# Piecewise loads, query-first landmarks and earlier denominators in a fused Nyström attention and FFN kernel

## The chip, the core and the metric

The kernel runs on one core of a Trainium2 chip. Its time is the device time in microseconds, taken over several runs; one further execution is profiled. The engines are named as the profile names them: PE is TensorE (matrix multiplications; PEld is its loading of weights), DVE is VectorE, ACT is ScalarE, POOL is GpSimd, SP is SyncE. SP, ACT and POOL also issue DMA transfers. [...]

## What is computed

```python
# per batch (8) and head (8): q, k, v are 576 x 64; m = 32 landmarks, each the mean of 18 rows
q_lm, k_lm = means of q and of k over groups of 18 rows
A  = softmax(q @ k_lm.T / 8)          # 576 x 32
Bm = softmax(q_lm @ k_lm.T / 8)       # 32 x 32
C  = softmax(q_lm @ k.T / 8)          # 32 x 576
Z  = Bm.T / (norm1(Bm) * norminf(Bm) + 1e-6)
for _ in range(6):
    Z = 2 * Z - Z @ Bm @ Z
attn = A @ Z @ C @ v
# then, over all 4608 tokens of width 512 (the heads side by side):
x = attn
h = ((x @ w1) * (x @ w2)) @ w3        # w1, w2: 512 x 1024; w3: 1024 x 1024
out = h @ w_out                       # w_out: 1024 x 512
```

All inputs and the output are float32.

## The kernel before

**Folding.** No step between `w3` and `w_out` is nonlinear, so the kernel first multiplies the two (`fold`, in float32) into `w34`. This is a generator of 64 steps, one matrix multiplication each; the program takes steps of it between the parts of the first batch's work. In the same manner `x @ w1` is never formed from the attention's output: the 32-column product `Z C v` of every head is multiplied by that head's rows of `w1` and `w2` (`project`, which gives G, tile `gt`), and the normalised `A` (tile `ahat`) is multiplied by G (`up`).

**Loading and turning.** `load_qk` brings q and k of a batch in as float16 through POOL's queue (96 partitions, 8 heads of 384 elements each); `load_v` brings v in as float32 through SP's queue. `turn_all` issues four DMA transposes on SP's queue, which give `qkT`: the 64 head dimensions of the two row halves on 128 partitions. `w1` and `w2` come in on partitions 0 to 63 of `wdup`; `double_weight` repeats them on partitions 64 to 127.

**Landmarks.** `landmarks` adds groups of rows of `qkT`, for k and for q, by four additions each. The results `parts` hold sums of one half of the rows on partitions 0 to 63 and of the other half on 64 to 127. `exchange` swaps the halves by two DMA transfers on SP into `other`, and `combine` adds the two into `lm`, a float16 tile that holds the full sums in both halves.

**Attention.** `attention` is a generator with 13 yields: `qbd` and the scores of Bm (`psB`); the scores of C in two parts (`scores_c`), whose exponentials `ect` POOL adds up (`presum`); the scores of A (`scores_a`) and the products with v (`cv`); then six iterations of the inverse on `chain`. In iterations 3, 4 and 5 a third of the reciprocals of A's denominators is taken (`inverted`); `mixed` makes `rmix` of them, and `normalise` multiplies them into A.

**The order of the work** is written out by hand: the functions issue instructions where the program calls them, and a tile pool's buffers add waits. The main loop runs over the eight batches. In batch b's iteration there come first the transposes and v's load of batch b+2; then the up-phase, eight pairs of `up` for batch b with one step of the attention of batch b+1 in each pair; then q's and k's load of batch b+3 and the landmarks of batch b+2; then the d-phase, which takes `down` (the product with `w34`, and the output stores on SP) 8 or 10 times. The d-phase steps on through the attention of batch b+1 and, in its last two places, through `project`:

```python
            steps(at if n < nd - 2 else proj)
            if n == 3 and b + 2 < B:
                exchange(sts[b + 2])
                combine(sts[b + 2])
```

PSUM is held as three buffers `big` of two banks, one `small` and one `acc`.

Of the kernel before, what the change touches and what calls it, by code (L numbers as in the profile page):

```python
# [8 lines left out]
FP32 = mybir.dt.float32  # L9
FP16 = mybir.dt.float16  # L10
AXF = mybir.ActivationFunctionType
ALU = mybir.AluOpType
AX = mybir.AxisListType

B = 8
H = 8
# [10 lines left out]
NP = 96  # L27
# [4 lines left out]
def kernel(  # L32
# [11 lines left out]
    nc = tc.nc  # L44
    consts = ctx.enter_context(tc.tile_pool(name="consts", bufs=1))
    wpool = ctx.enter_context(tc.tile_pool(name="wpool", bufs=1))
    pin = ctx.enter_context(tc.tile_pool(name="pin", bufs=2))
    pat = ctx.enter_context(tc.tile_pool(name="pat", bufs=2))
# [7 lines left out]
    def small():  # L56
        return psp.tile([128, 512], FP32, name="small", bufs=1)
# [7 lines left out]
    w34 = wpool.tile([128, 8, DM], FP16, name="w34")  # L65


    def load_qk(st, b):
        qkn = pin.tile([128, 2, H, 384], FP16, name="qkn")
        for t, src in ((1, k), (0, q)):  # L70
            nc.gpsimd.dma_start(out=qkn[0:NP, t, :, :],
                                in_=src[b].rearrange("h (p r) d -> p h (r d)", p=NP))
        st["qkn"] = qkn

    def load_v(st, b):
        vt = pin.tile([128, H, 384], FP32, name="vt")
        nc.sync.dma_start(out=vt[0:NP], in_=v[b].rearrange("h (p r) d -> p h (r d)", p=NP))
        st["vt"] = vt

    def load_weight(t, w):  # L80
        nc.gpsimd.dma_start(out=wdup[0:64, :, t, :], in_=w.rearrange("(h d) j -> d h j", d=D))

    def double_weight(t):
        nc.sync.dma_start(out=wdup[64:128, :, t, :], in_=wdup[0:64, :, t, :])

    def transposes(st, t, hs):
        if "qkT" not in st:
# [47 lines left out]
        return mask4, par, ones, eye, onesq, selc, lomask  # L135


    def landmarks(st, turned=None):

        st["parts"] = parts = pz.tile([128, 2, H, 32], FP32, name="parts")  # L140

        def sums(t, h0, n, eng, pool):
            x = st["qkT"][:, 1 - t, h0:h0 + n, :, :]
            tr = pool.tile([128, n, NP], FP32, name="tr", bufs=1)
            eng.tensor_tensor(out=tr, in0=x[:, :, 0, :], in1=x[:, :, 1, :], op=ALU.add)  # L145
            eng.tensor_tensor(out=tr, in0=tr, in1=x[:, :, 2, :], op=ALU.add)  # L146
            t3 = tr.rearrange("p h (l g) -> p h l g", g=3)
            o = parts[:, t, h0:h0 + n, :]
            eng.tensor_tensor(out=o, in0=t3[:, :, :, 0], in1=t3[:, :, :, 1], op=ALU.add)
            eng.tensor_tensor(out=o, in0=o, in1=t3[:, :, :, 2], op=ALU.add)  # L150

        sums(1, 0, H, nc.gpsimd, pat)
        if turned is None:
            sums(0, 0, H, nc.gpsimd, pat)
        else:
            sums(0, 0, 4, *turned)
            sums(0, 4, 4, *turned)


    def exchange(st):  # L160
        st["other"] = pat.tile([128, 2, H, 32], FP32, name="other", bufs=1)
        nc.sync.dma_start(out=st["other"][0:64], in_=st["parts"][64:128])
        nc.sync.dma_start(out=st["other"][64:128], in_=st["parts"][0:64])

    def combine(st):
        st["lm"] = lm = pat.tile([128, 2, H, 32], FP16, name="lm")
        nc.gpsimd.tensor_tensor(out=lm, in0=st["parts"], in1=st["other"], op=ALU.add)  # L167


    chain = [consts.tile([128, 2, 3, 32], FP32, name=f"chain{i}") for i in range(2)]  # L170
# [3 lines left out]

    def attention(st, bank=None, vbank=None):
        bank, vbank = bank or small, vbank or small
        qkT, vt, lm = st["qkT"], st["vt"], st["lm"]
        qbd = pat.tile([128, H, 2, 32], FP16, name="qbd")
        nc.vector.tensor_tensor(
# [1 line left out]
            in0=lm[:, 0, :, :].unsqueeze(2).to_broadcast([128, H, 2, 32]),  # L181
            in1=par.unsqueeze(1).unsqueeze(3).to_broadcast([128, H, 2, 32]),
            op=ALU.mult)
        psB = small()
        for qd in range(2):
            for h in range(4):
                nc.tensor.matmul(psB[32 * h:32 * h + 32, 32 * qd:32 * qd + 32],
                                 lm[0:64, 0, 4 * qd + h, :], lm[0:64, 1, 4 * qd + h, :],
                                 start=True, stop=True, tile_position=(0, 32 * h))
        ebm = pz.tile([128, 2, 32], FP32, name="ebm")  # L190
        nc.scalar.activation(out=ebm, in_=psB[:, 0:64].rearrange("p (a m) -> p a m", m=32),
# [33 lines left out]

        scores_c(0)
        es0 = presum(0)
        yield
        scores_c(1)
        es1 = presum(1)  # L230
# [92 lines left out]
        def inverted(i):  # L323
            sl = slice(QS // 3 * i, QS // 3 * (i + 1))
            nc.vector.reciprocal(out=psS[:, 1, sl], in_=psS[:, 0, sl])  # L325
# [21 lines left out]
        for it in range(6):  # L347
            last = it == 5
            old, new = chain[it % 2], chain[1 - it % 2]
            psI = bank() if it < 3 else small()  # L350
            for qd in range(2):
                for h in range(4):
                    sl = slice(32 * h, 32 * h + 32)
                    nc.tensor.matmul(  # L354
                        psI[sl, 64 * qd + 32 * last:64 * qd + 64], old[sl, qd, 0, :],
                        old[sl, qd, 2, :] if last else old[sl, qd, 0:3:2, :],
                        start=True, stop=True, tile_position=(32 * h, 32 * h))
            pv_ = psI[:, 0:128].rearrange("p (a c m) -> p a c m", a=2, m=32)
            if not last:
                nc.vector.tensor_tensor(out=new[:, :, 0:3:2, :], in0=old[:, :, 1:3, :], in1=pv_,  # L360
                                        op=ALU.add)
            else:
                y = pz.tile([128, 2, 32], FP32, name="y")
                nc.vector.tensor_tensor(out=y, in0=old[:, :, 2, :], in1=pv_[:, :, 1, :], op=ALU.add)
                ybd = pz.tile([128, 2, 4, 32], FP32, name="ybd")
                nc.vector.tensor_tensor(
                    out=ybd, in0=y.unsqueeze(2).to_broadcast([128, 2, 4, 32]),
                    in1=mask4.unsqueeze(1).to_broadcast([128, 2, 4, 32]), op=ALU.mult)
            if it == 0:
                cv(0, 1, psV0, es0)  # L370
                scaled(0, psV0)
            elif it == 1:
                psV1 = vbank()
                cv(1, 0, psV1)
            elif it == 2:
                cv(1, 1, psV1, es1)
                scaled(1, psV1)
                psS = denominators()
            else:
                inverted(it - 3)  # L380
            yield
        rmix = mixed()
        psZ = small()
        for qd in range(2):
            nc.tensor.matmul(psZ[:, 128 * qd:128 * qd + 128],
# [117 lines left out]
    sts = [dict() for _ in range(B)]  # L503

    def turn_all(b):
        for t in (1, 0):
            for h0 in (0, 4):
                transposes(sts[b], t, range(h0, h0 + 4))

    def steps(g, n=1):  # L510
        for _ in range(n):
            next(g, None)


    gate = consts.tile([128, 1], FP32, name="gate")
    with tc.tile_pool(name="pf", bufs=2) as pf:
# [19 lines left out]
            nc.tensor.matmul(psw[:, 0, 0:256], warm[:, 0:128], warm, start=True, stop=True)  # L536

        nc.gpsimd.tensor_copy(out=gate, in_=wof[:, 2, 0:1])
        load_qk(sts[0], 0)
        load_w3(2)  # L540
        mask4, par, ones, eye, onesq, selc, lomask = constants()
        fd = fold(pf, wof, w3f)
        steps(fd, 5)
        load_w3(3)
        turn_all(0)
        load_v(sts[0], 0)
        steps(fd, 8)
        load_w3(4)
        landmarks(sts[0])
        load_weight(0, moe_w1)  # L550
        load_weight(1, moe_w2)
        load_qk(sts[1], 1)
        steps(fd, 8)
        load_w3(5)
        exchange(sts[0])
        combine(sts[0])
        steps(fd, 8)
        load_w3(6)
        steps(fd, 6)
        double_weight(0)  # L560
        at = itertools.chain(attention(sts[0], vbank=lambda: big()[:, 0, :]), project(sts[0]))
        for n in range(28):
            steps(at)
            if n == 4:
                load_w3(7)
                double_weight(1)
                turn_all(1)
                load_v(sts[1], 1)
            if n == 17:
                landmarks(sts[1], (nc.vector, pf))  # L570
                load_qk(sts[2], 2)
                exchange(sts[1])
                combine(sts[1])
            steps(fd)
        steps(at, 30)
        steps(fd, 64)
# [4 lines left out]
    for b in range(B):  # L581
        st = sts[b]
        ab = st["ab"] = pab.tile([128, 8, S], FP16, name="ab")
        if b + 2 < B:
            turn_all(b + 2)
            load_v(sts[b + 2], b + 2)
        if b % 2 == 0:
            chunks = [[(b, ab, 128 * t, 128)] for t in range(4)]
        else:
            chunks = [[(b - 1, sts[b - 1]["ab"], 512, 64), (b, ab, 0, 64)]]  # L590
            chunks += [[(b, ab, 64 + 128 * t, 128)] for t in range(4)]
        for j in range(8):
            up(st, j, 0)
            steps(at)
            up(st, j, 1)
        if b + 3 < B:
            load_qk(sts[b + 3], b + 3)
        if b + 2 < B:
            landmarks(sts[b + 2])
        proj = project(sts[b + 1]) if b + 1 < B else iter(())  # L600
        hold = {}
        nd = 2 * len(chunks)
        for n in range(nd):
            bank = (lambda: big()[:, 0, :]) if n // 2 % 2 else acc
            down(chunks[n // 2], n % 2, hold, bank)
            steps(at if n < nd - 2 else proj)
            if n == 3 and b + 2 < B:
                exchange(sts[b + 2])
                combine(sts[b + 2])
        at = attention(sts[b + 2], acc) if b + 2 < B else iter(())  # L610


# [28 lines left out]
```

## Time and profile before

| what | value |
|---|---|
| time, median of 13 runs | 313.31 us (307.72 to 318.05) |
| the profiled execution's own time | 311.22 us |
| its span, first to last instruction | 309.4 us |
| TensorE busy | 285.4 us |
| VectorE, ScalarE, GpSimd busy | 167.9, 113.0, 126.9 us |
| mean granted TensorE clock | 0.983 |
| DMA, mean rate over the span | 164 GB/s |

The rows of the profile's groups read: line, engine, operation, output and inputs by the program's names, shapes, count, then total busy microseconds and mean nanoseconds of one, then idle time before it and what ended it. In the table of windows each line has the stretch, its length, the busy time and the number of instructions of PE, PEld, DVE, ACT and POOL, and at its end the granted clock, the share of the 16 DMA engines and GB/s. In the list of waits the three figures are microseconds in total, number of times and longest. "issue" stands where an engine waited for nothing that the profile shows. The DMA queues are q0 (issued by POOL), q1 (issued by SP), q10 (issued by ACT), q8 and q14 (instructions).

### The profile page before, as it was taken

The page shows a single profiled execution, that of the slowest core. Times are in us where ns is not written, and L with a number is a line of the kernel's source. Part 1 is how long each engine was busy: PE and PEld are TensorE (multiplying, and loading weights), DVE is VectorE, ACT ScalarE, POOL GpSimd, SP SyncE. Part 2 cuts the span into 40 slices and gives each one's busy share as a digit, 9 for nine tenths or more (in the row PEclk, how much of TensorE's full clock was granted, in tenths as well). Part 3 has the DMA queues.
Part 4 walks back from the last instruction along what each step waited for, and adds up shares of the span by engine and source line. Part 5 has one row for each costly group of instructions (what it writes and reads, how often), then busy time and mean ns, then how long its engine had stood idle before and what let it go on. Part 6 is the DMA issues. An engine that isn't in the chain of part 4 may idle for free.

```text
span 309.4 us, 8609 instructions
## 1 busy us (share of the span) xinstructions
PE 285.4 (92%) x3632; PEld 157.6 (51%) x3632; DVE 167.9 (54%) x408; ACT 113.0 (37%) x193; POOL 126.9 (41%) x141
## 2 busy tenths in 40 slices
PE   7999979999999899699999998997899999999994
PEld 5454435444366456344664663465446644654651
DVE  6111124369077658364865775485368764865720
ACT  1010003042162276125723742473047326723632
POOL 0209514008159429901793396149414931400000
PEclk9999979999999999899999999999799999999999
DMA  7999999999999578954999799599848934003114
GB/s 232 322 250 207 225 246 240 247 142 206 200 194 217 127 119 157 231 119 129 139 243 212 147 182 205 138 156 220 134 127 160 183 94 114 2 4 102 36 42 130
DMA packets 68424, 50.89 MB, mean 164 GB/s; under 512 B 39969, under 2 KB 58401, under 8 KB 68385
## 3 DMA queue, kind: packets, MB, share of 16 engines
q1 hardware_dynamic: 53696, 36.71, 54.7%
q0 software_dynamic: 13600, 11.54, 24.3%
q10 hardware_dynamic: 1088, 2.10, 1.9%
q8 instruction: 28, 0.46, 0.7%
q14 instruction: 12, 0.09, 0.1%
HBM read 38.80 MB, written 9.44 MB: 156 GB/s over the span
## 4 chain that ended last, share of the span: by engine, by line
PE 62%; DMA 11%; DVE 10%; ACT 6%; issue 5%; POOL 4%; SPq 1%; ACTq 0%; POOLq 0%; DVEq 0%
PE big L423 20%; PE acc L443 12%; PE big L443 7%; PE acc L497 5%; DMA other<-parts 5%; PE small L262 4%; PE small L354 3%; PE big L409 3%; PE acc L354 3%; DMA wof<-in_moe_w_out_dram 2%; DMA qkn<-in_k_dram 2%; DVE gt L415 2%; DVE ab L429 2%; PE big L339 2%; ACT ect L211 2%
## 5 line engine op out<-in xcount | busy, mean ns | idle before, releaser
L423 PE MATMUL big<-ahat,gt 128*128 128x288 f16 x512 | 75.4, 289 | 2.7 <-ACT a_sb L427 1.0
L423 PEld LDWEIGHTS <-gt 128*128 128x128 f16 x512 | 46.6, 98 | 21.8 <-issue 7.8
L429 DVE TENSOR_TENSOR ab<-a_sb,big 128x576 f16<-128x576 f16 x64 | 48.1, 752 | 16.8 <-PE big L423 8.6
L427 ACT CAST a_sb<-big 128x576 f16<-128x576 f32 x64 | 40.8, 638 | 39.2 <-PE big L423 39.2
L497 PE MATMUL acc<-wof,w3t 128*128 128x512 f32 x96 | 48.0, 621 | 1.0 <-DMA wof<-in_moe_w_out_dram 0.4
L443 PE MATMUL acc<-w,ab 128*128 128x512 f16 (+1 forms) x192 | 42.0, 393 | 0.0
L443 PEld LDWEIGHTS <-ab 128*128 128x128 f16 (+1 forms) x320 | 25.8, 102 | 28.7 <-issue 5.6
L145 POOL TENSOR_TENSOR tr<-qkT 128x768 f32<-128x768 f16 x15 | 24.6, 1641 | 31.2 <-DMA qkT<-qkn 30.6
L415 DVE TENSOR_SCALAR gt<-big 128x512 f16<-128x512 f32 x32 | 20.6, 686 | 27.7 <-ACT gt L413 27.7
L167 POOL TENSOR_TENSOR lm<-parts,other 128x512 f16<-128x512 f32 x8 | 10.1, 1268 | 55.7 <-DMA other<-parts 55.7
L218 POOL TENSOR_TENSOR t<-ect 96x384 f32<-96x384 f32 x16 | 16.0, 999 | 40.0 <-ACT ect L211 39.3
L443 PE MATMUL big<-w,ab 128*128 128x512 f16 x128 | 32.2, 381 | 0.0
L449 ACT ACTIVATE o_sb<-acc 128x512 f32<-128x512 f32 x20 | 11.9, 597 | 54.4 <-PE acc L443 53.3
L146 POOL TENSOR_TENSOR tr<-tr,qkT 128x768 f32<-128x768 f32 x15 | 24.8, 1652 | 1.2
L473 DVE COPY w3t<-big 128x512 f32<-128x512 f32 (+1 forms) x15 | 8.5, 583 | 29.9 <-PE big L465 29.8
L497 PEld LDWEIGHTS acc<-wof,w3t 128*128 128x128 f32 x96 | 16.8, 195 | 14.9 <-issue 11.9
L413 ACT ACTIVATE gt<-big 128x512 f16<-128x512 f32 x32 | 17.8, 595 | 6.5 <-PE big L409 6.5
L262 PE MATMUL small<-vt,ect 96*32 96x64 f32 x672 | 15.7, 225 | 3.1 <-issue 3.1
L409 PE MATMUL big<-wdup,zt 128*32 128x512 f16 x256 | 17.4, 382 | 0.1
L449 ACT ACTIVATE o_sb<-big 128x512 f32<-128x512 f32 x16 | 9.6, 597 | 21.7 <-PE big L443 18.3
L354 PEld LDWEIGHTS small<-chain 32*32 32x32 f32 x432 | 6.9, 105 | 15.5 <-DVE big L325 8.1
L497 PE MATMUL small<-wof,w3t 128*128 128x512 f32 x32 | 14.7, 593 | 0.0
(98 smaller groups left out, 326.0 us busy)
## 6 DMA issues: line engine op xcount, KB each, us to landing
vt<-in_v_dram SPq DMA_DIRECT2D x8, 1152.0 KB, 9.2
qkn<-in_k_dram POOLq DMA_DIRECT2D x8, 576.0 KB, 9.5
qkn<-in_q_dram POOLq DMA_DIRECT2D x8, 576.0 KB, 13.3
out_dram<-o_sb SPq DMA_DIRECT2D x24, 192.0 KB, 2.3
w3f<-in_moe_w_dram SPq DMA_DIRECT2D x6, 512.0 KB, 9.7
out_dram<-o_sb SPq DMA_DIRECT2D x24, 128.0 KB, 2.4
wof<-in_moe_w_out_dram ACTq DMA_DIRECT2D x4, 512.0 KB, 7.8
wdup<-in_moe_w_dram POOLq DMA_DIRECT2D x2, 1024.0 KB, 13.5
```

What stands on the lines that cost most here:

```text
L145: eng.tensor_tensor(out=tr, in0=x[:, :, 0, :], in1=x[:, :, 1, :], op=ALU.add)
L146: eng.tensor_tensor(out=tr, in0=tr, in1=x[:, :, 2, :], op=ALU.add)
L262: nc.tensor.matmul(psV[32 * h:32 * h + 32, 0:64], ects[qd][0:NP, h, r, :], vt[0:NP, 4 * qd + h, 64 * r:64 * r + 64], start=(r == 0), stop= ...
L354: nc.tensor.matmul(psI[sl, 64 * qd + 32 * last:64 * qd + 64], old[sl, qd, 0, :], old[sl, qd, 2, :] if last else old[sl, qd, 0:3:2, :], sta ...
L409: nc.tensor.matmul(psG[32 * h:32 * h + 32, n, :], zt[:, 4 * qd + h, :], wdup[:, 4 * qd + h, w, 512 * n:512 * n + 512], start=True, stop=Tr ...
L415: nc.vector.tensor_scalar(out=dst[:, 1, :], in0=psG[:, 1, :], scalar1=1.0 / ZS, scalar2=None, op0=ALU.mult)
L423: nc.tensor.matmul(p[:, c, 0:HS], st["g"][qd][:, w, 128 * j:128 * j + 128], st["ahat"][qd][:, c, :], start=(qd == 0), stop=(qd == 1))
L427: nc.scalar.copy(out=st["a_sb"], in_=p[:, :, 0:HS])
L429: nc.vector.tensor_tensor(out=st["ab"][:, j, :].rearrange("p (c s) -> p c s", c=2), in0=st["a_sb"], in1=p[:, :, 0:HS], op=ALU.mult)
L443: nc.tensor.matmul(pso[o:o + sz, :], ab[:, j, s0:s0 + sz], w34[:, j, :], start=(j == 0), stop=(j == 7), tile_position=(0, o))
L449: nc.scalar.activation(out=o_sb, in_=pso[:, :], func=AXF.Copy, scale=1.0 / (X64 * X64))
L497: nc.tensor.matmul(psW[j][:, :], turned[j, cc][:, c4, :], wof[:, c, :], start=(c == 0), stop=(c == 7))
```

## The change

- q is loaded, turned and summed ahead of k. In the main loop, `load_qk` and `load_v` become generators that issue four pieces: q in two and k in two, one piece ahead of each of the two long additions of a landmark sum, on POOL's queue; v in four, among the stores of the d-phase, on SP's queue.
- `exchange` and `combine` work on q and on k separately; `combine` moves from POOL to DVE, into `attention`. Bm is multiplied from q's full sums and k's partial sums `kp` (a float16 copy of `parts`) over all 128 partitions, and no exchange of k stands ahead of it.
- Two thirds of the reciprocals are taken in iteration 3, the last third and `mixed` in iteration 4.
- `project` takes the last but two and the last but one place of the d-phase.
- `double_weight` is 16 ScalarE copies, where it was two DMA transfers on SP.
- For the second batch, all sums are made on POOL, at the fifth step of the first batch's attention (n = 4), where they were made partly on DVE at n = 17.

```diff
+    def load_qk(st, b, n=8):
+        st["qkn"] = qkn = pin.tile([128, 2, H, 384], FP16, name="qkn")
+        for t, src in ((0, q), (1, k)):
+            for h in range(0, H, n):
+                yield
+                nc.gpsimd.dma_start(out=qkn[0:NP, t, h:h + n, :],
+                                    in_=src[b, h:h + n].rearrange("h (p r) d -> p h (r d)", p=NP))
+    def load_v(st, b, n=8):
+        st["vt"] = vt = pin.tile([128, H, 384], FP32, name="vt")
+        for h in range(0, H, n):
+            yield
+            nc.sync.dma_start(out=vt[0:NP, h:h + n],
+                              in_=v[b, h:h + n].rearrange("h (p r) d -> p h (r d)", p=NP))
-    def double_weight(t):
-        nc.sync.dma_start(out=wdup[64:128, :, t, :], in_=wdup[0:64, :, t, :])
+    def double_weight(t, h):
+        nc.scalar.copy(out=wdup[64:128, h, t, :], in_=wdup[0:64, h, t, :])
...
+    def landmarks(st, loads=iter(())):
         st["parts"] = parts = pz.tile([128, 2, H, 32], FP32, name="parts")
+        steps(loads)
+        for t in range(2):
+            x = st["qkT"][:, 1 - t]
+            tr = pat.tile([128, H, NP], FP32, name="tr", bufs=1)
+            steps(loads)
+            nc.gpsimd.tensor_tensor(out=tr, in0=x[:, :, 0, :], in1=x[:, :, 1, :], op=ALU.add)
+            steps(loads)
+            nc.gpsimd.tensor_tensor(out=tr, in0=tr, in1=x[:, :, 2, :], op=ALU.add)
...
+        st["kp"] = kp = pat.tile([128, H, 32], FP16, name="kp")
+        nc.gpsimd.tensor_copy(out=kp, in_=parts[:, 1])
...
+    def combine(st, t):
+        if t == 0:
+            st["lm"] = pat.tile([128, 2, H, 32], FP16, name="lm")
+        nc.vector.tensor_tensor(out=st["lm"][:, t], in0=st["parts"][:, t], in1=st["other"][:, t],
+                                op=ALU.add)
...
     def attention(st, bank=None, vbank=None):
+        combine(st, 0)
...
-                                 lm[0:64, 0, 4 * qd + h, :], lm[0:64, 1, 4 * qd + h, :],
+                                 lm[:, 0, 4 * qd + h, :], st["kp"][:, 4 * qd + h, :],
...
         es0 = presum(0)
+        combine(st, 1)
         yield
...
-            else:
-                inverted(it - 3)
+            elif it == 3:
+                inverted(0)
+                inverted(1)
+            elif it == 4:
+                inverted(2)
+                rmix = mixed()
             yield
-        rmix = mixed()
...
         for n in range(28):
             steps(at)
             if n == 4:
                 load_w3(7)
-                double_weight(1)
                 turn_all(1)
-                load_v(sts[1], 1)
-            if n == 17:
-                landmarks(sts[1], (nc.vector, pf))
-                load_qk(sts[2], 2)
-                exchange(sts[1])
-                combine(sts[1])
+                steps(load_v(sts[1], 1), 9)
+                landmarks(sts[1], load_qk(sts[2], 2, 4))
+                exchange(sts[1], 0)
+                exchange(sts[1], 1)
+            if 4 <= n < 8:
+                double_weight(0, 2 * n - 8)
+                double_weight(0, 2 * n - 7)
+            if 8 <= n < 12:
+                double_weight(1, 2 * n - 16)
+                double_weight(1, 2 * n - 15)
             steps(fd)
...
             turn_all(b + 2)
-            load_v(sts[b + 2], b + 2)
+        vs = load_v(sts[b + 2], b + 2, 2) if b + 2 < B else iter(())
+        steps(vs)
...
-        if b + 3 < B:
-            load_qk(sts[b + 3], b + 3)
+        qks = load_qk(sts[b + 3], b + 3, 4) if b + 3 < B else iter(())
         if b + 2 < B:
-            landmarks(sts[b + 2])
+            landmarks(sts[b + 2], qks)
+            exchange(sts[b + 2], 0)
...
             down(chunks[n // 2], n % 2, hold, bank)
-            steps(at if n < nd - 2 else proj)
+            if n % 2 == 1 or n == 0:
+                steps(vs)
+            steps(proj if n in (nd - 3, nd - 2) else at)
             if n == 3 and b + 2 < B:
-                exchange(sts[b + 2])
-                combine(sts[b + 2])
+                exchange(sts[b + 2], 1)
```

## The prediction

> **What bounds the kernel now.** I read the page first, then TensorE's idle times in the timeline, then the windows around the long ones.
>
> ```profile
> span 309.4 us, 8609 instructions
> ...
> PE 285.4 (92%) x3632; PEld 157.6 (51%) x3632; DVE 167.9 (54%) x408; ACT 113.0 (37%) x193; POOL 126.9 (41%) x141
> ...
> DMA  7999999999999578954999799599848934003114
> ...
> q8 instruction: 28, 0.46, 0.7%
> ...
> PE small L262 <- issue: 3.1, 1, 3.1
> PE small L187 <- POOL lm L167: 3.1, 2, 1.9
> PE small L267 <- issue: 2.8, 1, 2.8
> PE big L339 <- DVE rmix L332: 2.4, 7, 0.3
> ...
> PE big L423 <- DVE gt L415: 1.0, 4, 0.2
> ```
>
> TensorE is busy 92% of the span, so time comes only from its own holes. The two longest are put down to "issue": TensorE waited for nothing that the profile names. Their places:
>
> ```profile
> 101.77 0.43 PE L354 MATMUL small<-chain 32*32 32x64 f32 x16 [0.59 <-issue]
> ...
> 128.92 0.16 PE L267 MATMUL small<-ones,es 96*32 96x1 f32 x1 [2.81 <-issue]
> ...
> 188.41 0.29 PE L354 MATMUL small<-chain 32*32 32x64 f32 x2 [1.04 <-issue]
> ...
> 217.90 0.54 PE L262 MATMUL small<-vt,ect 96*32 96x64 f32 x10 [3.14 <-issue]
> ...
> 101.47:127.50 26.03, 22.93 (x382) 13.66 (x383) 16.90 (x38) 12.61 (x22) 14.95 (x17) 1.00 0.78 147
> 127.50:187.90 60.40, 56.72 (x892) 32.13 (x891) 38.51 (x89) 26.10 (x45) 33.26 (x36) 0.97 0.90 174
> 187.90:216.50 28.60, 25.41 (x382) 14.64 (x383) 17.24 (x40) 13.22 (x23) 15.18 (x17) 1.00 0.90 175
> ```
>
> The windows run from one such hole to the next. TensorE ran 382 + 383 = 765, then 1783, then 765 instructions: three, seven and three times 256, less a few lost records. Queue q8, "instruction", moved 28 packets of 16 KB, about as many as 3632 + 3632 instructions make blocks of 256. So TensorE ran out of program there. The block's transfer [...] stood behind loads: in the 4.3 us after 121.8 no q8 packet ran while q and k (q0) and v (q1) filled the engines; it started at 126.17, took 1.37 us, and TensorE went on at 128.92.
>
> ```profile
> q0 software_dynamic: 428, 0.33, 57.2%
> q1 hardware_dynamic: 359, 0.55, 47.6%
> 43.20:46.60 3.40, 3.40 (x23) 1.78 (x16) 1.28 (x5) 0.88 (x2) 0.00 (x0) 0.50 1.33 205
> 128.60:131.90 3.30, 2.98 (x22) 1.16 (x21) 1.33 (x3) 0.00 (x0) 2.73 (x3) 0.50 1.25 215
> 217.30:220.60 3.30, 2.70 (x35) 1.57 (x35) 1.14 (x3) 0.00 (x0) 3.06 (x4) 0.50 1.31 205
> ```
>
> The first two lines are the DMA of 121.8 to 126.1. The others show the second price: after the holes of 1.90, 2.81 and 3.14 us the granted clock (the third figure from the end) is 0.50. Each such stretch lasts 3.41 us in the trace and so costs about 1.7 us. After 1.19 and 1.04 us there was none.
>
> [...] under transposes alone it began 0.85 us after its block's start (114.3), but under both loads 4.4 us after (121.8) and 5.0 us (210.2). The measurement decides: what is already queued counts. [...]
>
> **The change, part by part.**
>
> Pieces. v's load goes from one issue beside q and k to four behind exchange and stores in the d-phase; q and k from two issues together to four, between GpSimd additions of 1.65 us. The bytes stay. Loading alone, q0 ran 621 packets in the 2.5 us from 130.0; a piece is 384 packets, so about 1.55 us. A fetch then waits at most about 1.6 us. How much wait a block covers: 4.4 us of wait gave 2.81 of hole (1.6 covered), 5.0 gave 3.14 (1.9), 3.4 gave 1.04 (2.4). So the four holes, 0.59 + 2.81 + 1.04 + 3.14 = 7.6 us, and two half-clock stretches, 3.4 us, go: 11.0 us. I leave 1.0 for a fetch that meets two transfers: gain 10.0, from 0 (fetches still late) to 11.0.
>
> Issues moved. On POOL four issues for two of 0.78 us: at most 1.6 us more, plus the copy kp at about 0.65 (the add L149 of that size), less 1.27 for lm. The additions end at about 133 instead of 131.5, and their results are first used in the next up-phase, after 146: nothing. On SP eight of its issues stand where three stood (v 4 for 1, exchange 4 for 2), at about 0.5 us: some 2.5 us more in a d-phase in which SP waited for o_sb (124.7 us over the span). Stores behind them feed nobody but o_sb's three buffers. The last v piece is issued near 141 and is read 9 us later; landing took 9.2 for a whole load. Cover gone would cost the missing microseconds in each of six batches.
>
> Start, first batch. The exchange of all sums was issued at 33.35 and landed at 41.56, and TensorE waited 1.90 us at 41.1 with a half-clock stretch after it: 3.6 us. Now q's sums (done at 27.7) are exchanged alone, behind v and w3 loads of 2.2 MB issued from 23.7, at 210 GB/s until about 34; kp needs no exchange. Bm's operands are there by 40: 3.6 gained. lm of k lands near 41.5, and scores_a wants it at 45.
>
> Start, against that: doubling w1 and w2 leaves the DMA (two issues of 12.9 us) and becomes 16 ScalarE copies of 64x1024. ScalarE took 383 ns for 256 elements and 595 for 512, 0.83 ns each, and two gt copies in a row took 1.09 us, so about 0.93 us per copy[...]. Fourteen stand ahead of zt, and two ahead of a w cast that frees psW. From about 48.3: 2 copies, cast 0.6, 12 copies, w3t 0.6, zt 0.4 ends at 63.4; TensorE, 3.6 us ahead, would want it at 60.9 for zt and 63.2 for the projection. The cast (50.8, wanted 50.0) costs 0.9, zt 0.6, the next cast 0.5, then gt follows late. The second projection, which needs gt copied out, then starts at about 51.5 + 16 copies = 67.0 and is through 1.2 earlier than before. Net gain of the start 1.2, between 3.6 (copies at 0.8) and a loss of 0.9 (copies at 1.1).
>
> Second batch's sums move from L570 (POOL and 6 us of DVE, exchange landing at 84.1) to n = 4 of the first batch, all on POOL; without the doubling's traffic k lands earlier. The hole of 1.19 at 84.4 goes: 1.2.
>
> Denominators. Reciprocals and rmix move ahead of y. Each batch's 0.34 us before L339 goes (7 x 0.34 = 2.4), but DVE's 0.46 + 0.31 + 0.36 now stand between the fifth chain add and y: they end at 163.5 where y began at 163.35, so y is some 0.1 late: gain 1.7.
>
> G sooner. The last down step follows the projection, and its 0.86 us cover gt: 4 x 0.25 = 1.0.
>
> combine moves from POOL to DVE in halves of 128x256, about 0.45 us each (L366 took 0.466). The first stands ahead of qbd, which at 172.93 began when the last gt ended; gt now ends about 0.9 sooner, so it is paid. The second stands ahead of ab in an up-phase where DVE is 80% busy: 0.1 x 7 = 0.7 lost.
>
> Bm contracts 128 rows against kp instead of 64: as many matmuls, as many columns, nothing. q ahead of k only orders these.
>
> Sum: -10.0 - 1.2 - 1.2 - 1.7 - 1.0 + 0.7 = -14.4 us. The profiled execution took 311.2 us (span 309.4): 296.8. The median shown is 313.3 (307.7 to 318.1); [...] I don't scale up: 297.0.
>
> **Rivals.**
> 1. Fetches stay late. For: seven more fetches began 3 us or more after their block did, with no hole, and transfers now fill quiet stretches. Against: no two long loads stand in the queues together. Without the 10.0: 306.8.
> 2. The pieces bunch up: SP runs ahead while stores wait for nothing, so v still meets q and k, the change not doing what it says. For: the first v piece follows q's exchange, near 126. Against: two stores of 1.1 us, each behind an o_sb, stand between the others. Half of the 10.0: 301.8.
> 3. Slower: the 16 copies hold zt and the casts. The start moves by 16c - 16.7 us, c being one copy; at 1.87 it eats the other 13.2 us of gains, and from there the kernel is slower. At 2.1: +16.9 instead of -1.2, so 314.9. Against: that is twice what the ScalarE rows give.
>
> **How the numbers follow.** Forecast 0.64, stalls stay 0.20, bunching 0.10, slow copies 0.06. The forecast's unknowns (start -2.4 to +2.1, fetches -1 to +3, combine to +1.5) give 292 to 304; rival 1 adds its 307. Range 290 to 307. About 1% is what this kernel's measurements can tell. Faster by over 1%: forecast, bunching and most of rival 1, 0.89; within 1% 0.05; slower 0.06.
>
> **What would show it.** Right: no "issue" hole above 0.6 us in TensorE's waits, granted clock 1.00 from 6 us on, L339 no longer waiting for rmix, L187 waiting for nothing long, wdup copies near 1 us. Wrong: holes of 3 us again at multiples of 256 instructions; ScalarE copies over 1.5 us with w casts and zt waited for; ab late behind combine.

## The result and the profile after

The changed kernel takes 297.49 us in the median of 11 runs (295.0 to 302.9), the kernel before 312.48 us in runs beside it: a ratio of 0.959, 95% interval 0.956 to 0.963. The runs of a kernel fall into a faster and a slower group: the two medians here are of all runs, but every ratio, its interval and the times of the experiments below are of the faster group (297.2 us for the changed kernel). The forecast was 297.0. The profiled execution took 296.65 us with a span of 294.9, against 311.22 and 309.4: 14.6 us less, where the sum of the steps gave 14.4.

The total is right. One step is not right for the reason given, and it is the largest. The experiments below are about that.

The page of the changed kernel, the lines that answer to those of before:

```profile
span 294.9 us, 8702 instructions
...
PE 279.9 (95%) x3632; PEld 155.4 (53%) x3632; DVE 169.2 (57%) x416; ACT 127.3 (43%) x209; POOL 130.7 (44%) x157
...
PEclk9999999999999999999999999999999999999999
...
q8 instruction: 28, 0.46, 0.7%
...
L92 ACT COPY wdup<-wdup 64x1024 f16<-64x1024 f16 x16 | 15.4, 1039 | 0.1
```

TensorE is busy for 95% of the span instead of 92%. No stretch of half clock is left after the warm-up (the granted clock is 1.00 from 5.40 us to the end), and the ScalarE copies cost 0.96 us each (15.4 us for 16; they overlap a little, so that the mean of one is listed as 1039 ns). Its list of waits (total, times, longest):

```profile
PE small L197 <- DVE lm L174: 2.2, 6, 0.5
...
PE acc L511 <- ACT w L514: 1.1, 2, 0.9
PE small L278 <- issue: 1.1, 1, 1.1
PE small L399 <- DVE ybd L377: 0.9, 3, 0.4
PE small L273 <- issue: 0.7, 1, 0.7
...
PE big L423 <- DVE zt L406: 0.5, 1, 0.5
```

Gone are rmix (2.4 us), gt (1.0), a_sb (1.0) and the long waits for lm (3.1). New are six short waits for lm. Two fetch holes are left, 1.07 and 0.71 us, and the windows between them show that they are of the same kind as before:

```profile
122.95:175.00 52.05, 50.41 (x778) 28.88 (x778) 37.85 (x87) 24.81 (x44) 29.22 (x36) 1.00 0.93 183
175.00:205.90 30.90, 29.50 (x502) 17.25 (x495) 20.87 (x49) 14.24 (x25) 19.22 (x22) 1.00 0.91 183
```

From the hole that ends at 122.95 to the one that ends at 205.90 TensorE ran 778 + 778 + 502 + 495 = 2553 instructions, ten times 256 less a few lost records. So the two begin where a block of instructions ends. The block of the first hole began at 117.53, and the next q8 packet started at 120.58, a wait of 3.05 us. What moved between 117.6 and 120.5:

```profile
q0 software_dynamic: 217, 0.17, 58.0%
q1 hardware_dynamic: 775, 0.19, 40.6%
```

These are the first piece of q and the end of the landmarks' transposes. One piece and the transposes kept a fetch for 3.05 us; the prediction had said 1.6 at most.

### The profile page after: what moved, and what is told of

It is laid out like the page before. It is cut to its first block, busy times and chain, and to the rows that moved or that the text cites. A ratio compares the mean times of both kernels' runs of the same rounds, so it can differ in the third digit from the quotient of the medians.

```text
span 294.9 us, 8702 instructions
## 1 busy us (share of the span) xinstructions
PE 279.9 (95%) x3632; PEld 155.4 (53%) x3632; DVE 169.2 (57%) x416; ACT 127.3 (43%) x209; POOL 130.7 (44%) x157
## 4 chain that ended last, share of the span: by engine, by line
PE 76%; DVE 9%; ACT 8%; issue 3%; DMA 3%; ACTq 0%; DVEq 0%
PE big L437 20%; PE acc L457 11%; PE acc L511 11%; PE big L457 7%; ACT wdup L92 5%; PE small L511 5%; PE small L273 5%; PE big L423 4%; DVE ab L443 3%; PE acc L365 3%; DMA wof<-in_moe_w_out_dram 3%; DVE gt L429 2%; PE small L365 2%; PE small L399 2%; PE big L479 1%
## 5 line engine op out<-in xcount | busy, mean ns | idle before, releaser
L437 PE MATMUL big<-ahat,gt 128*128 128x288 f16 x512 | 74.3, 287 | 0.8
L437 PEld LDWEIGHTS <-gt 128*128 128x128 f16 x512 | 46.5, 97 | 18.2 <-issue 2.2
L511 PE MATMUL acc<-wof,w3t 128*128 128x512 f32 x96 | 46.8, 608 | 2.0 <-ACT w L514 1.1
L457 PE MATMUL acc<-w,ab 128*128 128x512 f16 (+1 forms) x192 | 40.9, 381 | 0.0
L457 PEld LDWEIGHTS <-ab 128*128 128x128 f16 (+1 forms) x320 | 24.9, 100 | 29.1 <-issue 7.3
L154 POOL TENSOR_TENSOR tr<-qkT 128x768 f32<-128x768 f16 x16 | 26.3, 1646 | 26.0 <-DMA qkT<-qkn 25.7
L156 POOL TENSOR_TENSOR tr<-tr,qkT 128x768 f32<-128x768 f32 x16 | 26.4, 1650 | 0.4
L511 PEld LDWEIGHTS acc<-wof,w3t 128*128 128x128 f32 x96 | 16.3, 190 | 16.3 <-issue 11.9
L423 PE MATMUL big<-wdup,zt 128*32 128x512 f16 x256 | 17.6, 382 | 0.8 <-DVE zt L406 0.5
L92 ACT COPY wdup<-wdup 64x1024 f16<-64x1024 f16 x16 | 15.4, 1039 | 0.1
L514 ACT CAST w<-acc 128x512 f16<-128x512 f32 x6 | 3.5, 585 | 27.2 <-PE acc L511 27.2
L511 PE MATMUL small<-wof,w3t 128*128 128x512 f32 x32 | 14.7, 592 | 0.0
```

What stands on the lines that cost most here:

```text
L92: nc.scalar.copy(out=wdup[64:128, h, t, :], in_=wdup[0:64, h, t, :])
L154: nc.gpsimd.tensor_tensor(out=tr, in0=x[:, :, 0, :], in1=x[:, :, 1, :], op=ALU.add)
L156: nc.gpsimd.tensor_tensor(out=tr, in0=tr, in1=x[:, :, 2, :], op=ALU.add)
L423: nc.tensor.matmul(psG[32 * h:32 * h + 32, n, :], zt[:, 4 * qd + h, :], wdup[:, 4 * qd + h, w, 512 * n:512 * n + 512], start=True, stop=Tr ...
L437: nc.tensor.matmul(p[:, c, 0:HS], st["g"][qd][:, w, 128 * j:128 * j + 128], st["ahat"][qd][:, c, :], start=(qd == 0), stop=(qd == 1))
L457: nc.tensor.matmul(pso[o:o + sz, :], ab[:, j, s0:s0 + sz], w34[:, j, :], start=(j == 0), stop=(j == 7), tile_position=(0, o))
```

## The experiments

Two words for what follows. The *wait* of a block is the time from its first instruction to the start of the q8 packet that brings the next block, both taken from the trace. Which packet that is I read from the holes: at the five fetch holes of 0.7 us and more in the traces of the two kernels TensorE went on 1.38 to 1.47 us after a packet's end (at 128.92 in the kernel before, after the packet that ended at 127.54). The *hole* is TensorE's idle time at the end of the block. The longest holes of the kernel before, and both of the changed one, lie at the ends of two *short blocks*, of 4.2 to 4.6 us of work, which begin at about TensorE's instructions 2241 and 4801; a batch's loads are issued about when they begin. Elsewhere waits of up to 5 us mostly fall on blocks of 6 to 14 us, which cover them: 4.04 us on the block that began at 128.92 in the kernel before, of some 13 us, left no hole.

Theory 1, the prediction's: whole loads delay the fetch, pieces don't. Rival theory 2: what counts is which loads were issued ahead of the fetch, and so how the loads fall against the blocks.

### e1: the pieces alone

The kernel before, with the four pieces of v, q and k as in the change; k stays ahead of q and all else stays.

```
-            load_v(sts[b + 2], b + 2)
+        vs = load_v(sts[b + 2], b + 2, 2) if b + 2 < B else iter(())
...
-            load_qk(sts[b + 3], b + 3)
+        qks = load_qk(sts[b + 3], b + 3, 4) if b + 3 < B else iter(())
...
+            if n % 2 == 1 or n == 0:
+                steps(vs)
```

> The kernel before with the four pieces of q, k and v alone (k still ahead of q; start, exchange, denominators, project and doubling untouched). Theory 1 (late instruction fetches are the main loss and the pieces cure them): the 'issue' holes of TensorE at multiples of 256 instructions shrink from 7.6 us to under 2 us, no half-clock stretch after the start, and the median falls by 7 to 10 us against before. Rival (the fetches are late for another reason, and the gain came from the start and the d-phase): within 2 us of before, holes of 2 to 3 us as before.

Measured: 303.47 us, ratio 0.974 (0.968 to 0.979). Its waits:

```profile
PE small L197 <- POOL lm L177: 6.0, 5, 2.7
PE big L349 <- DVE rmix L342: 2.4, 7, 0.3
PE big L433 <- ACT a_sb L437: 1.6, 6, 0.4
...
PE small L272 <- issue: 0.3, 1, 0.3
```

The fetch holes fall from 7.6 to 0.3 us. But waits for GpSimd's lm, 3.1 us before, become 6.0, one of 2.73 with a half-clock stretch behind it. So in the kernel before, pieces do cure the fetch holes, by about the predicted amount.

### e2: the changed kernel with whole loads

```
-        vs = load_v(sts[b + 2], b + 2, 2) if b + 2 < B else iter(())
-        steps(vs)
+        if b + 2 < B:
+            steps(load_v(sts[b + 2], b + 2), 9)
...
-        qks = load_qk(sts[b + 3], b + 3, 4) if b + 3 < B else iter(())
+        if b + 3 < B:
+            steps(load_qk(sts[b + 3], b + 3), 9)
...
```

> The changed kernel with whole loads in the main loop: v beside the transposes, q and k together ahead of the landmark additions. Theory 1: 7 to 10 us slower than the changed kernel, 305 to 307 us, with holes of 1 to 3 us between instructions that stand multiples of 256 apart, and the clock at 0.50 after the long ones. Rival: 298 us, holes under 1.1 us.

Measured: 297.1 us, ratio 0.954 (0.950 to 0.958), the same as the changed kernel. Theory 1 falls as a reason for the changed kernel's time: without pieces nothing is lost. The waits of e2 still show three fetch holes, none of them long:

```profile
PE small L365 <- issue: 0.9, 1, 0.9
PE small L278 <- issue: 0.7, 1, 0.7
PE small L273 <- issue: 0.6, 1, 0.6
```

### e3: the blocks moved in the kernel before

64 more tiny matmuls among those that warm up, that is 128 more TensorE instructions (the page lists as many of PEld as of PE, 3632 each).

```
+        for _ in range(64):
+            nc.tensor.matmul(psw[:, 0, 0:16], warm[:, 0:128], warm[:, 0:16], start=True, stop=True)
```

> The kernel before with 64 more small warming multiplications (128 instructions of TensorE) ahead of everything, some 2 to 4 us at the start. If the holes belong to the instruction blocks, they stay at counts of 193 plus a multiple of 256 and so move 128 instructions earlier in the program, to other lines and with other sizes. If they belong to a place in the program (a wait that the profile doesn't name), they stay before the same lines (the products with v and es of the late up-phase) and keep sizes near 3 us.

Measured: 312.99 us, one run. The holes move to other lines and stay at every 256th instruction: between the four below the trace has 1784, 1784 and 764 instructions of TensorE, seven, seven and three times 256 less a few lost records. From its timeline:

```profile
98.28 0.33 PE L262 MATMUL small<-vt,ect 96*32 96x64 f32 x9 [1.65 <-issue]
...
159.47 0.41 PE L423 MATMUL big<-ahat,gt 128*128 128x288 f16 x2 [3.31 <-issue]
...
219.18 0.31 PE L354 MATMUL small<-chain 32*32 32x64 f32 x8 [1.20 <-issue]
...
246.32 0.31 PE L317 MATMUL big<-eat,onesq 128*32 128x144 f16 x2 [3.45 <-issue]
```

L423 is up, which had no fetch hole before: the holes belong to the blocks and not to a place in the program. Their sum, 9.9 us with a fifth of 0.26, isn't smaller.

### e4: q's combine on GpSimd

The six waits of L197 are for the combine on VectorE that the prediction called paid. Here q's half of it runs on GpSimd in the d-phase.

```
-        nc.vector.tensor_tensor(out=st["lm"][:, t], in0=st["parts"][:, t], in1=st["other"][:, t],
-                                op=ALU.add)
+        eng = nc.vector if t else nc.gpsimd
+        eng.tensor_tensor(out=st["lm"][:, t], in0=st["parts"][:, t], in1=st["other"][:, t],
+                          op=ALU.add)
...
-        combine(st, 0)
         qkT, vt, lm = st["qkT"], st["vt"], st["lm"]
...
                 exchange(sts[b + 2], 1)
+                combine(sts[b + 2], 0)
```

> The changed kernel with q's combine on GpSimd in the d-phase; k's stays on VectorE. The changed kernel's trace has six waits of the first scores' multiplications for combine, 2.2 us in all. Theory: they go, 295.3 us, 2 us faster than the changed kernel. Rival: qbd, which still follows the last gt on VectorE, becomes what is waited for, and the time stays within 0.7 us of 297.5.

Measured: 297.99 us, ratio 0.956 (0.949 to 0.964): no gain. The waits for lm are gone, and a fetch hole has grown:

```profile
PE small L278 <- issue: 1.9, 1, 1.9
PE small L399 <- DVE ybd L377: 1.5, 3, 0.7
...
PE small L273 <- issue: 0.7, 1, 0.7
```

and 3.41 us at half clock follow the hole of 1.95 us. What the waits cost came back as a fetch.

### e5 and e6: the changed kernel with its blocks moved

The 64 matmuls of e3 in the changed kernel (e5), and in e2, the one with whole loads (e6).

> The changed kernel with 64 more tiny matmuls among the warm-up ones at the start (128 more TensorE instructions), so that each block of 256 begins half a block earlier in the program; no data change. Theory 'pieces': loads in pieces keep every fetch short, so wherever a block begins nothing is missed: within 1 us of the changed kernel (296.5 to 298.5), fetch holes together under 2 us. Theory 'phase': what counts is how a block's start falls against the loads, and the changed kernel has a lucky fall: shifted, it gets fetch holes of 3 to 8 us back and takes 300 to 305.

> The changed kernel with whole loads of v, q and k in the main loop (as e2) and the same 64 tiny matmuls. Theory 'pieces': e2 was a lucky fall, and shifted it loses 5 to 10 us: 302 to 307, well above e5. Theory 'phase' with pieces that do nothing at all: the same as e5 within 1.5 us. Theory 'stores and projection moved': what cures is that the last down-projections no longer run beside the loads; then it stays at 297 like e2.

Measured: 298.39 us, ratio 0.956 (0.951 to 0.961), and 297.27 us, 0.956 (0.948 to 0.964). Fetch holes sum to 2.5 and 1.6 us. So e2 was no lucky fall, and pieces do nothing measurable in the changed kernel with the blocks in either of two positions. Of the theories in these texts only the last, that the stores, the projection and what hangs on them moved, is not refuted so far; e7 and e11 look at it.

### e7: the projection moved alone

The kernel before with the projection after the third and second last half down-projections.

```
-            steps(at if n < nd - 2 else proj)
+            steps(proj if n in (nd - 3, nd - 2) else at)
```

> The kernel before with one edit: the two halves of the projection of the next batch run after the third and second last half down-projections, and the last attention step comes after the last. Prediction's sum for this edit: 1.0 us less (the four waits of up for gt at 0.25 us), so 310.5. Theory 'phase': the blocks and loads fall otherwise against each other, part of the 11 us of fetch holes and half clock goes: 302 to 308.

Measured: 304.29 us, ratio 0.980 (0.973 to 0.986): a good 6 us less, as theory 'phase' had it, where the prediction's sum gave 1.0. The waits for gt and a_sb are gone from its profile (2.0 us), but not the fetch holes:

```profile
PE small L267 <- issue: 2.9, 1, 2.9
...
PE small L354 <- issue: 2.1, 3, 0.8
...
PE small L262 <- issue: 1.1, 1, 1.1
PE acc L354 <- DVE chain L304: 0.4, 1, 0.4
```

6.0 us in all, against 7.6. In waits the edit is worth twice its predicted 1.0, since a_sb's hung on it too; beyond that it takes away part of the holes. Most of the rest lies in the clock: its trace has one half-clock stretch (from 85.97) where the kernel before has three, and none follows the hole of 2.88 us (the last section shows how that can be). So this one edit, priced at 1.0, gives about half of the whole change (0.980 against 0.959), some 3.4 us of it by the clock (an estimate: two stretches fewer, at 1.7 us each).

### e11: in the kernel before, q and k issued later

```
         sums(1, 0, H, nc.gpsimd, pat)
+        mid()
...
-            load_qk(sts[b + 3], b + 3)
...
-            landmarks(sts[b + 2])
+            landmarks(sts[b + 2], None, lambda: b + 3 < B and load_qk(sts[b + 3], b + 3))
```

> The kernel before, with the whole loads of k and q in the main loop issued after GpSimd's sums of k instead of ahead of them, some 5 us later; loads stay whole, nothing else moves. Theory 'what is in front of the fetch': the blocks 2241, 4033 and 4801 begin ahead of these loads, so their holes (2.81, 1.04, 3.14 us, with two half-clock stretches of 1.7 us each lost) fall to under 1 us each and the time to 302 to 306. Theory 'size': only shorter loads help, the holes just move to other blocks and it stays at 309 to 313.

Measured: 309.34 us, ratio 0.996 (0.991 to 1.000): nothing. That spoke against what I expected of theory 2, until one looks at which load is left. Its timeline for SP and POOL, then TensorE's first instruction after the hole:

```profile
111.69 6.67 SPq L90 DMA_TRANSPOSE qkT<-qkn  x4
118.45 0.81 SPq L77 DMA_DIRECT2D vt<-in_v_dram  x1
...
123.69 0.79 POOL L71 DMA_DIRECT2D qkn<-in_k_dram  x1
124.47 0.77 POOL L71 DMA_DIRECT2D qkn<-in_q_dram  x1
...
127.56 0.16 PE L268 MATMUL small<-ones,es 96*32 96x1 f32 x1 [2.48 <-issue]
```

The short block began at 120.73. k and q were issued 3 us after that, so they were not in front of its fetch; v, issued by 119.26, was. The fetch still waited 4.47 us. v's whole load (1152 KB) was enough.

### e10: nothing but the transposes in front

e9 (below) with each piece of q and k issued one place later between GpSimd's additions; v is in pieces, the first of them much later.

```
-        steps(loads)
         for t in range(2):
...
             nc.gpsimd.tensor_tensor(out=o, in0=o, in1=t3[:, :, :, 2], op=ALU.add)
+        steps(loads)
         st["kp"] = kp = pat.tile([128, H, 32], FP16, name="kp")
```

> e9 with every piece of q and k issued one place later in GpSimd's sums (the first after the first addition of q's sums, the last after k's), so about 2 us later. The theory that what a fetch waits for is the loads issued before it: at the two short blocks (TensorE instructions 2241 and 4801) no q piece is in front any more, the waits of 2.8 to 3.9 us fall to 1 us or less and both holes are gone, 2 to 3 us less than e9. Rival: what is left in front there is the four transposes of the landmarks' batch, issued last on SP before the block began; then the waits stay at 2 to 3 us, the holes at 0.5 to 1 us, and it is within 1 us of e9.

Measured: 296.18 us, ratio 0.952 (0.949 to 0.956). SP, POOL and TensorE at the same short block:

```profile
113.42 6.62 SPq L98 DMA_TRANSPOSE qkT<-qkn  x4
...
120.75 0.69 POOL L74 DMA_DIRECT2D qkn<-in_q_dram  x1
...
120.49 0.54 PE L273 MATMUL small<-vt,ect 96*32 96x64 f32 x24
```

The block began at 120.57, the q piece was issued after it, and the wait was 1.00 us; at the other short block it was 0.92. No fetch hole is left in the whole run: the first theory named in its expectation holds for the holes, and the transposes alone are worth at most about 1 us. It does not hold for the time, which is 0.4 us below e9's and not 2 to 3. The short blocks of seven kernels side by side; a figure after a load is when its issue ended against the block's first instruction, the transposes stand in front in all of them (in e10, at the second block, the last of the four is still being issued):

| kernel | in front at the first short block | wait, hole | in front at the second | wait, hole |
|---|---|---|---|---|
| before | k -1.02, v -0.92, q -0.25 | 4.41, 2.81 | v -0.41, k -0.28 | 5.00, 3.14 |
| e11 | v -1.47 | 4.47, 2.48 | v -0.38 | 5.13, 3.14 |
| e7 | k -0.86, q -0.10 | 4.73, 2.88 | k -0.11 | 3.26, 1.05 |
| e2 | q -0.44 | 2.62, 0.72 | q -0.11 | 2.50, 0.64 |
| after | q piece -0.54 | 3.05, 1.07 | q piece -0.13 | 2.81, 0.71 |
| e1 | v piece -1.80, k piece -1.28 | 2.18, 0.06 | k piece -0.29 | 2.46, 0.34 |
| e10 | nothing | 1.00, none | nothing | 0.92, none |

With all of v, or k and q together, in front a fetch waited 4.4 to 5.1 us; with one of k and q, or pieces, 2.2 to 3.3; with nothing but the transposes, 1 us. The table leaves out e4, e8, e9 and e12: with a q piece in front of the first short block as in the changed kernel (-0.50 to -0.54) the fetch waited 3.51, 3.88, 3.10 and 4.97 us there. For the holes of 0.6 us and more in the table the hole is the wait plus 2.4 to 2.8 us (0.9 to 1.4 of it the transfer) less the block's own time. The waits of 0.92 and 1.00 us left none.

### e12: denominators as before

```
-            elif it == 3:
-                inverted(0)
-                inverted(1)
-            elif it == 4:
-                inverted(2)
-                rmix = mixed()
+            else:
+                inverted(it - 3)
             yield
+        rmix = mixed()
```

> The changed kernel with the reciprocals of the denominators and rmix as before: one third of the reciprocals after each of the last three rounds, rmix after the loop. By the prediction's sum this gives back 1.9 us (the 0.34 us wait of normalise for rmix in seven of the eight batches): 299.2. Rival: the wait only replaces the one of L399 for ybd, or fetch holes move by as much: 296.5 to 298.

Measured: 302.62 us, ratio 0.970 (0.963 to 0.977): 5 us lost, not 1.9. From its waits:

```profile
PE small L278 <- issue: 3.1, 1, 3.1
PE big L350 <- DVE rmix L343: 2.4, 7, 0.3
```

rmix costs the 2.4 us of before. The rest is a fetch hole of 3.09 us with half clock after it, at the first short block. In front of that fetch stood the same q piece as in the changed kernel, at the same -0.54, and yet it waited 4.97 us. At the second short block it waited 1.43. What differs in the trace is the transposes: the last one's issue ended 0.10 us before the block began and not 0.47, and in the stretch from 1 to 4 us after the block's start SP's queue moved 522 packets in e12 and 79 in the changed kernel. First e12 (119.1 to 122.1), then the changed kernel (118.5 to 121.5):

```profile
q1 hardware_dynamic: 522, 0.13, 87.6%
q0 software_dynamic: 194, 0.15, 60.1%
...
q0 software_dynamic: 476, 0.35, 97.7%
q1 hardware_dynamic: 79, 0.01, 3.6%
```

So the same piece in front went with waits of 3.05 and 4.97 us and doesn't fix their length. Whether the transposes that ran beside it lengthened the second is not shown; no run tests it.

### e8 and e9: weights doubled by DMA

e8 is the changed kernel with the two doubling DMAs on SP as before, in place of the ScalarE copies; e9 is e8 with e4's edit.

```
-        nc.scalar.copy(out=wdup[64:128, h, t, :], in_=wdup[0:64, h, t, :])
+        nc.sync.dma_start(out=wdup[64:128, :, t, :], in_=wdup[0:64, :, t, :])
...
```

> The changed kernel with the upper half of the weights written by two DMAs on SP as before, in place of 16 ScalarE copies. Prediction's start sum: copies give back 2.4 of 3.6 us that the start gains, so without them 2.4 us less, 295.1. Rival: the DMAs (1 MB beside the transposes and loads of the start) delay the fetches and the landmarks of the second batch by as much or more: 297.5 to 301, with holes at the start (PE time 40 to 90 us).

> The changed kernel with the two edits of e8 and e4 together: weights doubled by DMA, and q's landmarks combined on GpSimd in the d-phase. Sum: e8's 295.9 less the six waits of 0.28 to 0.46 us for lm at the first products of each batch (2.2 us) gives 293.7 if the fetch holes stay as in e8 (2.7 us and one half-clock stretch); 291 to 292 if those are smaller. Rival: as in e4 the time won only brings the short blocks of instructions under the loads, and it stays at 295.5 to 297.5.

Measured: 295.91 us, ratio 0.951 (0.944 to 0.958), and 296.57 us, 0.956 (0.950 to 0.962). In e8's trace TensorE waits for the w cast ahead of the same L511 from 73.45, 1.8 us sooner than with the copies (75.27), and gives most of it back here:

```profile
82.79 0.23 PE L197 MATMUL small<-kp,lm 128*32 128x32 f16 x8 [1.48 <-DVE lm L174]
```

That is the second batch's lm, whose exchange lands later than in the changed kernel: VectorE, which waited for it, began the combine at 82.3 us and not at 74.0. The copies cost the start about what they save here. e8's median lies near its forecast of 295.1, though its interval meets the changed kernel's; e9 gains nothing over e8, misses its 293.7 and lies within its rival's 295.5 to 297.5. No version clearly beats the changed kernel; e10 and e8 come nearest, with intervals that overlap its own.

## Why the prediction was right, and where its steps were not

- **Fetch holes, predicted -10.0.** 11.0 us of holes and half clock became 1.8, so -9.2: the size is right. The step that failed is "a fetch then waits at most about 1.6 us": with a piece in front those of the short blocks were 1.4 to 5.0 (2.81 and 3.05 in the changed kernel itself). And the pieces are not what the changed kernel needs: e2 and e6 lack them and lose nothing. Pieces cure the kernel before (e1: 0.3 us of holes for 7.6); in the changed kernel something else has cured it already.
- **What that is.** In e2 the transposes started 7.5 us ahead of the first short block instead of 9.0, as also in e7. The last half down-projection, whose stores stand ahead of the transposes on SP, now follows the projection. So v's issue ends 0.48 us after the block began and no longer 0.92 before it. In e7 that is not enough, since k and q both still lie in front (4.73 us); in e2 only q does (2.62). So the move of the projection is shown to shift v. The loads of GpSimd shift for another reason. In e7, as in the kernel before, TensorE waits 0.41 us for chain just ahead of the first short block (the last line of e7's waits); in e2, e4 and the changed kernel this wait is gone, and the block begins that much earlier against the loads: the first of them ends at -0.44 instead of -0.86. At the second short block, where e7 has no such wait, it ends at -0.11 in both. q's combine on VectorE is not the reason: without it (e4) q's piece ends at -0.53, with it at -0.54. Nor are the denominators or the copies, since e12 and e8 lack the wait too. q ahead of k, kp and k's combine are left; no run tests them alone. The prediction counted the move of the projection at 1.0 gained, the order of q and k at nothing, and missed what they do to the transfers.
- **Rivals 1 and 2** had a true part. Fetches did stay late, and two holes remain; but the other late ones meet longer blocks: 3.51 us on the one that began at 122.95, of some 11 us, left no hole. And v's first piece, issued at 123.77, still meets those of k (122.47 and 124.76).
- **Start, predicted -1.2.** The second projection began at 67.14 (67.0 predicted, 68.37 before) and one copy took 0.96 us (the prediction's 16 copies from 51.5 to 67.0 come to 0.97 each). The w cast cost 0.88 (0.9) and zt 0.47 (0.6). Rival 3 is out. Before's start hole of 1.90 us is not constant: 2.08 in e1, 1.19 in e11, none in e3 and e7.
- **Second batch's lm, -1.2.** The second up of the first pair began at 83.22 instead of 85.71: 2.5 us, of which 1.2 are the start and 1.2 this. As predicted.
- **Denominators, -1.7.** rmix's 2.4 us went, and ybd's waits rose from 0.3 to 0.9: -1.8.
- **G sooner, -1.0.** gt's 1.0 went. a_sb's six waits, another 1.0, went with it; the prediction didn't count them.
- **combine, +0.7.** Mis-sized: "so it is paid" was wrong. In six batches TensorE waited 0.28 or 0.46 us for the first half, 2.2 us. The 0.7 had been put on the second half, for ab; the changed kernel's list has no wait for ab.
- **Bm over 128 rows, predicted nothing.** One multiplication took 183 ns in the median (L197), and 180 over 64 rows in the kernel before (L187).

These terms sum to -9.2 - 2.5 - 1.8 - 2.0 + 2.2 = -13.3 of the 14.6 us; 1.3 are not accounted for. The errors, 0.8 too much for the holes and 1.5 too little for combine, were made up by a_sb and this rest: that the sum came within 0.2 us is luck.

## What to carry to other kernels

Where TensorE idles for "issue", count instructions between the holes; if they are multiples of 256, look for which transfers were issued ahead of the short block's fetch, and shift those past it. In these runs a load's place against the block mattered more than its size: a whole q of 576 KB at -0.44 kept the fetch for 2.62 us (e2), a piece of 288 KB at -0.54 for 3.05 (the changed kernel). And edits that moved an engine by under half a microsecond changed a fetch's wait: at the first short block from 3.05 us to 3.51 in e4 and to 4.97 in e12, the hole from 1.07 to 1.95 and to 3.09, with half clock after it. With that half clock at an estimated 1.7 us this cost 2.6 and 3.7 us, more than the waits that the edits were about (2.2 and 2.4). Price such an edit by its traces, not by its own instructions alone.

## What the runs showed of the hardware

- Half clock after a hole is not a matter of its length alone. 1.65 (e3), 1.90, 1.95 (e4), 2.81, 3.14 and 3.45 us (e3) were followed by 3.41 us at half clock; 2.08 (e1), 2.88 (e7), 3.31 (e3) and 3.45 us (e10) were not. In e3, after the hole that ended at 159.47, then after the one that ended at 246.32:

```profile
159.50:162.90 3.40, 3.40 (x46) 1.68 (x46) 1.58 (x4) 0.55 (x1) 2.07 (x3) 1.00 1.05 164
...
246.30:249.70 3.40, 3.38 (x24) 1.30 (x27) 0.75 (x1) 0.00 (x0) 0.51 (x1) 0.51 0.02 5
```

  In these traces it went by where the hole lay. In one trace the half-clock stretches began at whole multiples of 3.413 us from each other: 43.19, 128.52 and 217.27 in the kernel before (25 and 26 times), 99.57 and 246.35 in e3 (43 times), 128.14 and 216.89 in e11 (26 times). Cut each trace into windows at these edges, from 8 us on to 3 us before the end: in the fourteen traces every window in which TensorE was idle for 1.89 us or more was followed by half clock, none with less than 1.65 us was, and between the two both occurred (1.65 in e3 was, 1.88 in e3 was not). In the kernel before, the window up to 128.52 has 2.41 us of idle time. In e10 an edge cuts the hole of 3.45 us into 1.72 and 1.73, and the clock stayed at 1.00:

```profile
125.11:128.52 3.41, 1.00 (x48) 0.75 (x47) 0.80 (x2) 0.64 (x1) 3.17 (x4) 1.00 1.17 232
128.52:131.93 3.41, 3.01 (x22) 1.16 (x21) 1.33 (x3) 0.00 (x0) 2.81 (x3) 0.50 1.25 216
...
62.76:66.17 3.41, 1.69 (x14) 0.69 (x6) 1.29 (x2) 1.45 (x3) 0.00 (x0) 1.00 1.55 154
66.17:69.58 3.41, 1.67 (x18) 0.85 (x19) 0.38 (x1) 1.01 (x2) 0.00 (x0) 1.00 0.95 172
69.58:72.99 3.41, 3.41 (x12) 1.69 (x12) 0.91 (x2) 0.07 (x1) 3.01 (x3) 1.00 1.01 170
```

  So in these traces whether a hole of 2 to 3.45 us was followed by half clock, some 1.7 us more, went by where an edge fell in it, and the edges fell elsewhere in each: an edge at 128.52 in the kernel before, at 128.14 in e11.

- VectorE was held up while GpSimd worked. In e10 the same combine of 128x256 that takes 0.42 us in the changed kernel took 1.18, and with 1.19 us of waiting for its exchange it made ab late, so that TensorE waited 1.51 us at L437. First VectorE, then GpSimd:

```profile
86.69 1.18 DVE L175 TENSOR_TENSOR lm<-parts,other 128x256 f16<-128x256 f32 x1 [1.19 <-DMA other<-parts]
...
86.60 0.99 POOL L228 TENSOR_TENSOR t<-ect 96x384 f32<-96x384 f32 x1 [3.22 <-ACT ect L221]
```

The combine began just after GpSimd's addition and ended 0.28 us after it. It took 0.76 us longer than in the changed kernel, a little less than the 0.90 that were left of the addition when it began. The changed kernel shows the like at L299 (`cs`, 128x64): all eight began while a GpSimd addition ran, took 0.38 to 0.99 us and ended 0.05 us after that addition; in the kernel before, the one that began together with the addition, at 48.97, took 0.20 us. So part of what e10 won at the fetches went into waits for ab (4.5 us at L437 in its profile).
